# Short convolution and gated feed-forward on one core: the last eviction of a unit shared between two engines, and another order of turns in the last unit

## The chip, the cores and the metric

The kernel runs on one core of one Trainium2 chip. The metric is the device time of one execution in microseconds, and less is better. TensorE (PE) multiplies matrices into PSUM, ScalarE (ACT) and VectorE (DVE) read PSUM, GpSimd (POOL) works on SBUF alone, and SyncE (SP) issues most of the DMA transfers.

## The reference

The input is `x` with 8 batches of 4096 tokens and 192 channels. The first stage is a causal convolution over 7 tokens whose taps are a softmax over 7 weights, one set for each of 8 heads of 24 channels. The second stage is a feed-forward layer with 1536 hidden channels and a gate:

```python
out = np.einsum('hk,bskhg->bshg', softmax(weight), x_unf)   # x_unf: 7 shifted copies of x
x = out.reshape(B * S, D)                                   # 32768 x 192
gate = np.maximum(x @ w_gate, 0.0)
val = x @ w_val
return (gate * val @ w_out)                                 # 32768 x 192
```

## The kernel before

The schedule is written out by hand: every engine executes its instructions in the order in which the program issues them. The 8 batches are taken as 4 pairs, two streams `st` that lie on the upper and the lower 64 partitions. A unit is 1024 tokens of one pair (two windows of 512), and there are 16 units, `u` from 0 to 15.

A unit has two phases on TensorE. First `gate_val` runs for each of its two windows. For each of 12 slices `f` of the hidden channels, 6 matmuls with `Wg` and 6 with `Wv` (line 505) fill two PSUM tiles. ScalarE applies the relu to the gate tile (line 514), and VectorE multiplies the result by the value tile into `hT` (line 515). Each PSUM tile `ps` is two banks of 512 fp32, and the pool has four of them, used in rotation. A slice takes two tiles, so slice `f` reuses the tiles of slice `f - 2`: the value tile of slice 2 is the one that VectorE reads for slice 0.

Then `project` multiplies `hT` by `Wo`. The unit has four halves `i` (two windows, two streams), each with one PSUM tile in which four blocks `q` of 128 tokens by 192 channels lie, two to a bank. Each half is done in two turns (`half_pass`, matmuls on line 534). A turn is 96 matmuls, each with 64 of the 128 rows, and runs over the pairs of blocks (0, 2) and (1, 3), one after the other. The two turns exchange the upper and the lower rows, so that matmuls of different rows never write a bank at the same time. Between the first and the second turn of a half an empty instruction on SyncE (line 547) marks that the first is over. The order of (half, turn) is a list in `project` (lines 590 to 594), with its own form for the last unit. Unit 0 does whole halves with all 128 rows (line 554).

After the second turn of a half, `evict` calls `put`: ScalarE copies the whole tile (768 fp32 a partition, line 567) to an `out_s` buffer, of which there are three, and SyncE issues a store of 384 KB (line 568). The last half of the last unit (`final`) takes three tiles, and is evicted in three pieces on ScalarE and VectorE, with three stores.

While TensorE projects unit `u`, VectorE and ScalarE convolve for unit `u + 2` if there is one. In a unit from 1 to 13, VectorE has 18 instructions on line 481 and 5 products on line 454 in `lane_rest`, all issued ahead of `project`. ScalarE has 16 products on line 452 (`product`), spread over the halves in front of their evictions: 5, 5, 5 and 1. GpSimd adds the products (line 458), and its first addition for the next unit is issued at the start of the unit.

Of the kernel before, what the change touches and what calls it, by code (L numbers as in the profile page):

```python
# [15 lines left out]
def kernel(  # L16
# [12 lines left out]
    nc = tc.nc  # L29

    B, S, D = x.shape
# [4 lines left out]
    NB = B // 2  # L36
# [3 lines left out]
    WIN = 512  # L40
# [66 lines left out]
    def stage(p0, rows, st, n_st, jj, n):  # L107
        at = room[p0 : p0 + rows, 0, 0, 0:1]
        dims = [[D * GSUB, n_st], [D, n], [1, D]]
        return bass.AP(  # L110
            tensor=at.tensor,
            offset=at.offset + D * (GSUB * st + jj),
            ap=[at.ap[0]] + [d for d in dims if d[1] > 1],
        )
# [3 lines left out]
    def body(st):  # L118
# [13 lines left out]
        out=spaced[:, :, GAP : GAP + SEG],  # L132
        in_=ones[0:SUB, 0 : KW * SEG].rearrange("p (k s) -> p k s", k=KW),
# [8 lines left out]
        out=stage(PAD, DSUB, 0, 2, 0, 1),  # L142
        in_=bass.AP(
            tensor=x.tensor, offset=x.offset, ap=[[D, DSUB], [NB * S * D, 2], [1, D]]
        ),
# [53 lines left out]
    def summed(out, step, n, at):  # L199
# [15 lines left out]
        out=mx[:], in_=wr[:], axis=mybir.AxisListType.X, op=ALU.max, negate=True  # L215
# [9 lines left out]
        out=over[:],  # L225
# [10 lines left out]
        out=spread[0:SUB, 0, 0:H],  # L236
# [7 lines left out]
    with nc.allow_low_precision("products with one and zero"):  # L244
        nc.vector.tensor_tensor(
            out=diag[:],
# [6 lines left out]
    for a in range(2):  # L253
        for b in range(NSEG):
            nc.tensor.matmul(
                out=(bps, spread)[a][:, a, HB * SEG * b : HB * SEG * (b + 1)],
# [12 lines left out]
    for h in range(H):  # L269
        r = G * h  # L270
        while r < G * (h + 1):
            c, n = r // 64, min(64 - r % 64, G * (h + 1) - r)
            nc.sync.dma_start(
                out=tap[r % 64 : r % 64 + n, c, :],
                in_=taps[h : h + 1, :].unsqueeze(1).to_broadcast([1, n, KW]),
# [166 lines left out]
    def shifted(u, c, k, lane):  # L442
        o = HALO - KW + 1 + k
        if lane:
            return xrs[u][:, c, 128 * TDVE + o : 128 * TDVE + o + LPOOL]
        return xrs[u][:, c, o : o + LDVE]

    def product(engine, u, c, k):
        out = prods[u][:, k, c, :]
        in_, scale = shifted(u, c, k, 1), tap[:, c, k : k + 1]  # L450
        if engine is nc.scalar:
            engine.activation(out=out, in_=in_, func=ACTF.Copy, scale=scale)  # L452
        else:
            engine.tensor_scalar(out=out, in0=in_, scalar1=scale, scalar2=None, op0=ALU.mult)  # L454
# [63 lines left out]
    def slots(final):  # L518
        wide = [psum.tile([128, 2, 512], FP, name="ps")]
        if not final:  # L520
            return wide, [wide[0][:, q // 2, D * (q % 2) : D * (q % 2) + D] for q in range(4)]
        wide += [psum.tile([128, 2, 512], FP, name="ps") for _ in range(2)]
        return wide, [t[:, n, 0:D] for t, n in zip((wide[0], wide[1], wide[0], wide[2]), (0, 0, 1, 0))]

    SYNC = mybir.DependencyInfo(mybir.DependencyClass.Sync, mybir.DependencyReason.DATA)

    def half_pass(h, st, outs, final, turn, after):


        for n, pair in enumerate(((0, 2), (1, 3))):  # L530
            for f in range(NFF):
                for r in range(2):
                    q = pair[r ^ turn]
                    mm = nc.tensor.matmul(  # L534
                        out=outs[q],
                        lhsT=h[64 * r : 64 * r + 64, f, st, 128 * q : 128 * (q + 1)],
                        rhs=Wo[64 * r : 64 * r + 64, f, :],
                        start=(turn == 0 and f == 0 and (n == 0 or final)),
                        stop=(turn == 1 and f == NFF - 1),
                        tile_position=(64 * r, 0),  # L540
                        skip_group_check=True,
                    )
                    if after is not None:
                        tc.add_manual_dep(mm.ins, after.ins.name, SYNC, reason="same banks, other rows")
                        after = None
        if turn == 0:
            done = nc.sync.nop()
            tc.add_manual_dep(done.ins, mm.ins.name, SYNC, reason="first turn over")
            return done

    def half_whole(h, st, outs):
        for q in range(4):
            for f in range(NFF):
                nc.tensor.matmul(  # L554
                    out=outs[q],
                    lhsT=h[:, f, st, 128 * q : 128 * (q + 1)],
                    rhs=Wo[:, f, :],
                    start=(f == 0),
                    stop=(f == NFF - 1),
                )  # L560

    def put(copy, queue, src, row, n, gap, os_=None):
        if os_ is None:
            os_ = opool.tile([128, 4, D], FP, name="out_s")
        m = src.shape[1] if len(src.shape) == 3 else 1
        dst = os_[:, 0:n, :].rearrange("p (a b) d -> p a (b d)", a=m)
        copy(out=dst, in_=src if len(src.shape) == 3 else src.unsqueeze(1))  # L567
        queue.dma_start(
            out=bass.AP(
                tensor=out.tensor,  # L570
                offset=out.offset + row * D,
                ap=[[D, 128], [gap * D, n], [1, D]],
            ),
            in_=os_[:, 0:n, :],
        )

    def evict(wide, row0, final):
        if not final:
            put(nc.scalar.copy, nc.sync, wide[0][:, :, 0 : 2 * D], row0, 4, 128)
            return  # L580
        ends = apool.tile([128, NCH, LDVE], FP, name="acc")
        o = [ends[:, c, 0 : LDVE].rearrange("p (b d) -> p b d", d=D) for c in range(NCH)]
        put(nc.scalar.copy, nc.sync, wide[0][:, :, 0:D], row0, 2, 256, o[0])
        put(nc.vector.tensor_copy, nc.sync, wide[1][:, 0, 0:D], row0 + 128, 1, 128, o[1])
        put(nc.scalar.copy, nc.scalar, wide[2][:, 0, 0:D], row0 + 384, 1, 128, o[2])

    def project(u, hs, work):
        bp, w0 = u * UNIT // S, u * UNIT % S // WIN
        at, done = {}, {}
        order = [(0, 0), (1, 0), (0, 1), (2, 0), (1, 1), (3, 0), (2, 1), (3, 1)]  # L590
        if u == 0:
            order = [(i, 2) for i in range(4)]
        if u == NUNIT - 1:
            order = [(0, 0), (1, 0), (0, 1), (1, 1), (2, 0), (3, 0), (2, 1), (3, 1)]
        for i, turn in order:
            final = u == NUNIT - 1 and i == 3
            h, st = hs[i // 2], i % 2
            if turn != 1:
                at[i] = slots(final)
            if turn:  # L600
                for c, k in work[i]:
                    product(nc.scalar, u + 2, c, k)
            if turn == 2:
                half_whole(h, st, at[i][1])
            else:
                done[i] = half_pass(h, st, at[i][1], final, turn, done.get(i))
            if turn:
                evict(at[i][0], (bp + NB * st) * S + WIN * (w0 + i // 2), final)
            if u == 0 and i == 0:
                conv(3, 0)  # L610
                conv(3, 1)
# [12 lines left out]
    for u in range(NUNIT):  # L624
# [29 lines left out]
        if u + 2 < NUNIT:  # L654
# [4 lines left out]
            cut = [0, 4, 8, 12, 16] if u == 0 else [0, 5, 10, 15, 16]  # L659
            work = [todo[a:b] for a, b in zip(cut, cut[1:])]  # L660
        project(u, hs, work)


# [28 lines left out]
```

## Time and profile before

| | us |
|---|---|
| three runs | 770.40, 770.37, 769.57 |
| median | 770.37 |
| the profiled execution | 769.82 |
| its span, first to last instruction | 767.8 |
| outside the span | 2.02 |

| engine | busy us | share |
|---|---|---|
| TensorE matmul | 762.1 | 99% |
| VectorE | 684.8 | 89% |
| ScalarE | 604.5 | 79% |
| GpSimd | 369.9 | 48% |

The granted TensorE clock was full speed throughout. The four times lie 0.83 us, or 0.11%, apart. In the profile's views a row begins with the start and the duration in microseconds, counted from the start of the span. In the timeline, brackets give the idle time of the engine just before the row and what ended it. A row with a count merges that many instructions.

### The profile page before, as it was taken

What the parts mean: (1) busy time and instruction counts of PE and PEld (TensorE: products, weight loads), DVE (VectorE), ACT (ScalarE), POOL (GpSimd) and SP (SyncE); (2) the same over time, 40 slices, a digit from 0 to 9 for tenths busy, and PEclk for the clock granted to TensorE, in tenths of its full rate; (3) what the DMA queues carried; (4) which work ended last, traced back from release to release, by engine and by line L of the source; (5) the groups of instructions that cost most, each with busy time, mean ns of one, the idle gap of its engine ahead of it and who ended that gap; (6) DMA issues with size and microseconds to landing.
All of it is one profiled execution on the core that took longest, in us unless ns stands there. A gap on an engine that the chain in (4) does not pass through costs nothing.

```text
span 767.8 us, 24842 instructions
## 1 busy us (share of the span) xinstructions
PE 762.1 (99%) x10842; PEld 527.1 (69%) x10842; DVE 684.8 (89%) x729; ACT 604.5 (79%) x733; POOL 369.9 (48%) x212
## 2 busy tenths in 40 slices
PE   8999999999999999999999999999999999999998
PEld 4495675957759576585866858567595775957757
DVE  6999999989999999999999999999998999995590
ACT  6797887888878788887888878788787887874571
POOL 8608638093470926619166290843909346090000
PEclk9999999999999999999999999999999999999999
DMA  8966727180372704428054271712719131200202
GB/s 121 128 107 118 91 89 90 49 126 6 97 80 69 106 23 98 60 85 94 23 111 46 85 91 44 113 24 85 93 44 117 21 94 37 65 22 22 64 2 84
DMA packets 131809, 56.11 MB, mean 73 GB/s; under 512 B 96741, under 2 KB 131701, under 8 KB 131701
## 3 DMA queue, kind: packets, MB, share of 16 engines
q1 hardware_dynamic: 90789, 38.85, 24.4%
q0 software_dynamic: 40768, 15.59, 19.0%
q8 instruction: 84, 1.38, 0.8%
q14 instruction: 24, 0.20, 0.1%
q10 hardware_dynamic: 144, 0.10, 0.0%
HBM read 31.68 MB, written 25.17 MB: 74 GB/s over the span
## 4 chain that ended last, share of the span: by engine, by line
PE 98%; DMA 1%; DVE 0%; ACT 0%; issue 0%; POOL 0%; POOLq 0%
PE ps L505 65%; PE ps L534 31%; PE ps L554 2%; DMA x_h<-in_x_dram 1%; PE ps L333 0%; PE ps L358 0%; DVE hT L515 0%; ACT gr L514 0%; DVE acc L567 0%; POOL spaced L129 0%; POOLq L676 0%
## 5 line engine op out<-in xcount | busy, mean ns | idle before, releaser
L515 DVE TENSOR_TENSOR hT<-gr,ps 128x1024 f16<-128x1024 f16 x384 | 468.4, 1221 | 60.0 <-ACT gr L514 33.4
L514 ACT ACTIVATE gr<-ps 128x1024 f16<-128x1024 f32 x384 | 393.2, 1024 | 100.2 <-PE ps L505 100.2
L458 POOL TENSOR_TENSOR prods<-prods 128x1344 f32<-128x1344 f32 x70 | 212.4, 3034 | 309.8 <-ACT out_s L567 279.3
L505 PE MATMUL ps<-xc,Wv 64*128 64x512 f16 x2304 | 317.3, 376 | 0.2 <-DVE hT L515 0.2
L505 PE MATMUL ps<-xc,Wg 64*128 64x512 f16 x2304 | 317.3, 376 | 0.0
L534 PEld LDWEIGHTS <-hT 64*128 64x128 f16 x5760 | 238.5, 94 | 3.1
L534 PE MATMUL ps<-Wo,hT 64*128 64x192 f16 x5760 | 240.3, 243 | 0.0
L505 PEld LDWEIGHTS <-Wv 64*128 64x128 f16 x2304 | 138.5, 94 | 111.1 <-issue 3.0
L505 PEld LDWEIGHTS <-Wg 64*128 64x128 f16 x2304 | 128.2, 94 | 116.5 <-issue 0.3
L481 DVE SCALAR_TENSOR_TENSOR acc<-x_r,tap,acc 128x576 f32<-128x576 f16 x210 | 154.3, 810 | 1.6 <-ACT acc L469 1.6
L452 ACT ACTIVATE prods<-x_r,tap 128x448 f32<-128x448 f16 x222 | 130.4, 663 | 0.0
L567 ACT COPY out_s<-ps 128x768 f32<-128x768 f32 x63 | 50.6, 803 | 54.3 <-PE ps L534 44.4
L414 POOL DMA_DIRECT2D x_e<-in_x_dram x56 | 45.2, 819 | 3.3 <-POOL x_p L433 3.3
L433 POOL COPY x_p<-x_e 128x1728 f16<-128x1728 f16 x28 | 44.7, 1626 | 1.8 <-DMA x_e<-in_x_dram 1.8
L458 POOL TENSOR_TENSOR xc<-prods 128x1344 f16<-128x1344 f32 x14 | 42.4, 3026 | 1.1
L481 DVE SCALAR_TENSOR_TENSOR xc<-x_r,tap,acc 128x576 f16<-128x576 f16 x42 | 31.7, 809 | 0.0
L469 ACT ACTIVATE acc<-x_r,tap 128x576 f32<-128x576 f16 x42 | 29.4, 767 | 0.0
L454 DVE TENSOR_SCALAR prods<-x_r,tap 128x448 f32<-128x448 f16 x72 | 27.3, 445 | 0.0
L554 PE MATMUL ps<-Wo,hT 128*128 128x192 f16 x192 | 16.2, 246 | 0.0
L554 PEld LDWEIGHTS <-hT 128*128 128x128 f16 x192 | 15.9, 98 | 0.0
L567 DVE COPY acc<-ps 128x192 f32<-128x192 f32 x1 | 0.4, 357 | 14.2 <-PE ps L534 14.2
L333 PEld LDWEIGHTS <-x_h 110*32 110x32 f16 (+3 forms) x240 | 3.2, 92 | 2.6 <-issue 1.3
(51 smaller groups left out, 59.2 us busy)
## 6 DMA issues: line engine op xcount, KB each, us to landing
out_dram<-out_s SPq DMA_DIRECT2D x63, 384.0 KB
x_e<-in_x_dram POOLq DMA_DIRECT2D x34, 192.0 KB, 6.2
x_e<-in_x_dram POOLq DMA_DIRECT2D x22, 240.0 KB, 5.3
x_r<-x_p SPq DMA_TRANSPOSE x126
Wo<-in_moe_w_out_dram POOLq DMA_DIRECT2D x1, 576.0 KB, 10.1
x_h<-in_x_dram POOLq DMA_DIRECT2D x2, 240.0 KB, 7.6
x_h<-in_x_dram POOLq DMA_DIRECT2D x2, 210.0 KB, 5.7
x_h<-in_x_dram POOLq DMA_DIRECT2D x2, 192.0 KB, 8.0
```

The lines of the kernel that those rows point to most:

```text
L414: nc.gpsimd.dma_start(out=xe[:, j : j + n, st, :, :].rearrange("p j c r -> p j (c r)"), in_=bass.AP(tensor=x.tensor, offset=x.offset + (b ...
L433: nc.gpsimd.tensor_copy(out=xp[:, :, :, st, :], in_=xe[:, :, st, :, :])
L452: engine.activation(out=out, in_=in_, func=ACTF.Copy, scale=scale)
L458: nc.gpsimd.tensor_tensor(out=pr[:, 0] if k < KW - 1 else xc[u][:, :, LDVE:UNIT], in0=pr[:, 0], in1=pr[:, k], op=ALU.add,)
L469: nc.scalar.activation(out=accs[u][:, c, :], in_=shifted(u, c, 0, 0), func=ACTF.Copy, scale=tap[:, c, 0:1],)
L481: nc.vector.scalar_tensor_tensor(out=xc[u][:, c, 0:LDVE] if k == KW - 1 else acc[:, c, :], in0=shifted(u, c, k, 0), scalar=tap[:, c, k : k ...
L505: nc.tensor.matmul(out=pss[i][:, st, :], lhsT=W[64 * st : 64 * st + 64, c, 128 * f : 128 * (f + 1)], rhs=xcb[64 * st : 64 * st + 64, c, WI ...
L514: nc.scalar.activation(out=gr[:], in_=pss[0][:], func=ACTF.Relu)
L515: nc.vector.tensor_tensor(out=h[:, f], in0=gr[:], in1=pss[1][:], op=ALU.mult)
L534: mm = nc.tensor.matmul(out=outs[q], lhsT=h[64 * r : 64 * r + 64, f, st, 128 * q : 128 * (q + 1)], rhs=Wo[64 * r : 64 * r + 64, f, :], sta ...
L554: nc.tensor.matmul(out=outs[q], lhsT=h[:, f, st, 128 * q : 128 * (q + 1)], rhs=Wo[:, f, :], start=(f == 0), stop=(f == NFF - 1),)
L567: copy(out=dst, in_=src if len(src.shape) == 3 else src.unsqueeze(1))
```

## The change

Two things change. In units 1 to 14, the eviction of half 3 becomes two copies of one bank each (384 fp32 a partition): the first on ScalarE, the second on VectorE. One store of 384 KB still takes the buffer out. In the last unit the order of turns becomes (0,0) (1,0) (0,1) (2,0) (1,1) (2,3) (3,0) (2,4) (3,1), in place of (0,0) (1,0) (0,1) (1,1) (2,0) (3,0) (2,1) (3,1). Turns 3 and 4 are the two parts of half 2's second turn, the pair (0, 2) and the pair (1, 3), 48 matmuls each. Each part has an eviction of its own on ScalarE, over the columns of its two blocks in both banks, and a store of 192 KB. Half 3 is evicted as before.

```diff
-    def half_pass(h, st, outs, final, turn, after):
-        for n, pair in enumerate(((0, 2), (1, 3))):
+    def half_pass(h, st, outs, final, turn, after, part=(0, 1)):
+        for n in part:
+            pair = (n, n + 2)
             for f in range(NFF):
...
-        copy(out=dst, in_=src if len(src.shape) == 3 else src.unsqueeze(1))
+        src = src if len(src.shape) == 3 else src.unsqueeze(1)
+        copies = copy if isinstance(copy, tuple) else (copy,)
+        step = m // len(copies)
+        for j, one in enumerate(copies):
+            one(out=dst[:, step * j : step * j + step], in_=src[:, step * j : step * j + step])
         queue.dma_start(
...
-    def evict(wide, row0, final):
+    def evict(wide, row0, final, shared):
         if not final:
-            put(nc.scalar.copy, nc.sync, wide[0][:, :, 0 : 2 * D], row0, 4, 128)
+            copy = (nc.scalar.copy, nc.vector.tensor_copy) if shared else nc.scalar.copy
+            put(copy, nc.sync, wide[0][:, :, 0 : 2 * D], row0, 4, 128)
             return
...
         if u == NUNIT - 1:
-            order = [(0, 0), (1, 0), (0, 1), (1, 1), (2, 0), (3, 0), (2, 1), (3, 1)]
+            order = [(0, 0), (1, 0), (0, 1), (2, 0), (1, 1), (2, 3), (3, 0), (2, 4), (3, 1)]
         for i, turn in order:
...
-            if turn != 1:
+            if turn in (0, 2):
                 at[i] = slots(final)
-            if turn:
+            if turn in (1, 2):
                 for c, k in work[i]:
                     product(nc.scalar, u + 2, c, k)
+            if turn > 2:
+                n = turn - 3
+                half_pass(h, st, at[i][1], final, 1, done.pop(i, None), (n,))
+                put(
+                    nc.scalar.copy,
+                    nc.sync,
+                    at[i][0][0][:, :, D * n : D * n + D],
+                    (bp + NB * st) * S + WIN * (w0 + i // 2) + 128 * n,
+                    2,
+                    256,
+                )
+                continue
...
-                evict(at[i][0], (bp + NB * st) * S + WIN * (w0 + i // 2), final)
+                evict(at[i][0], (bp + NB * st) * S + WIN * (w0 + i // 2), final, u > 0 and i == 3)
```

## The prediction, made before the changed kernel was run

> **What bounds the kernel now.** I read the page first. Its engine line says that TensorE leaves almost nothing free:
>
> ```profile
> PE 762.1 (99%) x10842; PEld 527.1 (69%) x10842; DVE 684.8 (89%) x729; ACT 604.5 (79%) x733; POOL 369.9 (48%) x212
> ```
>
> The chain of waits shows where the rest can be. It runs on TensorE from unit to unit, and ends after its last matmul:
>
> ```profile
> 106.48 31.14 PE ps L505 x288
> ...
> 717.10 31.13 PE ps L505 x288
> 748.23 15.87 PE ps L534 x384
> 764.10 0.02 issue
> 764.12 0.36 DVE acc L567
> ```
>
> Each `gate_val` phase from unit 2 to unit 15 takes 31.13 or 31.14. A change that leaves TensorE's matmuls alone can win only what these phases hold above the matmuls' own pace, and the end after 764.10. So I read the timeline where unit 1 passes to unit 2, engine by engine:
>
> ```profile
> 105.35 1.90 DVE L454 TENSOR_SCALAR prods<-x_r,tap 128x448 f32<-128x448 f16 x5
> 108.32 3.71 DVE L515 TENSOR_TENSOR hT<-gr,ps 128x1024 f16<-128x1024 f16 x3 [1.07 <-ACT gr L514]
> ...
> 106.56 0.80 ACT L567 COPY out_s<-ps 128x768 f32<-128x768 f32 x1 [0.66 <-ACT prods L452]
> 107.26 1.03 ACT L514 ACTIVATE gr<-ps 128x1024 f16<-128x1024 f32 x1
> 108.46 1.02 ACT L514 ACTIVATE gr<-ps 128x1024 f16<-128x1024 f32 x1 [0.17 <-PE ps L505]
> 109.75 1.02 ACT L514 ACTIVATE gr<-ps 128x1024 f16<-128x1024 f32 x1 [0.27 <-PE ps L505]
> 111.10 1.02 ACT L514 ACTIVATE gr<-ps 128x1024 f16<-128x1024 f32 x1 [0.32 <-PE ps L505]
> ...
> 108.25 0.81 PE L505 MATMUL ps<-xc,Wv 64*128 64x512 f16 x6
> 108.90 0.81 PE L505 MATMUL ps<-xc,Wg 64*128 64x512 f16 x6
> 109.59 0.82 PE L505 MATMUL ps<-xc,Wv 64*128 64x512 f16 x6
> ```
>
> Groups of six matmuls start 0.65 apart, except that the value group of slice 2 starts 0.69 after its gate group. It needs the PSUM tile that VectorE reads for slice 0. That multiplication starts at 108.32 and lasts 1.22 (page: mean 1221 ns), so it ends at 109.54, just when the group is due (109.55). It is late because the relu of slice 0 is: ScalarE copies half 3 from 106.56, and takes the relu up at 107.26. A relu that TensorE alone releases starts 0.85 after its gate group (108.90 to 109.75). For slice 0, whose group starts at 106.31, that is 107.16, so the copy costs 0.10 of delay. What TensorE loses shows on ScalarE: relus are 1.295 apart (111.10 to 137.00 is 20 steps), but 109.75 to 111.10 is 1.35, so 0.055. The chain agrees: 24 steps of 1.295 are 31.08 of the 31.13. All 14 phases after units 1 to 14 have this length.
>
> For the end, the timeline and the stretches:
>
> ```profile
> 762.13 0.80 ACT L567 COPY out_s<-ps 128x768 f32<-128x768 f32 x1 [5.14 <-PE ps L534]
> ...
> 763.62 1.23 SPq L568 DMA_DIRECT2D out_dram<-acc  x2
> ...
> 764.44 0.39 ACTq L568 DMA_DIRECT2D out_dram<-acc  x1
> ```
>
> ```profile
> 763.00:763.80 0.80, 0.80 (x24) 0.80 (x21) 0.00 (x0) 0.48 (x1) 0.00 (x0) 1.00 0.00 0
> ...
> 764.00:765.00 1.00, 0.07 (x2) 0.00 (x0) 0.36 (x1) 0.32 (x1) 0.00 (x0) 1.00 1.01 326
> 765.00:766.00 1.00, 0.00 (x0) 0.00 (x0) 0.00 (x0) 0.00 (x0) 0.00 (x0) 1.00 1.03 321
> ...
> 766.20:766.40 0.20, 0.00 (x0) 0.00 (x0) 0.00 (x0) 0.00 (x0) 0.00 (x0) 1.00 0.68 208
> ```
>
> The last two columns are the DMA engines' share and GB/s. From about 763.9 to 766.34 all sixteen are full. They carry half 2 (384 KB) and half 3 (192 + 96 + 96 KB): 786 KB at 325 GB/s is 2.42 us. The last stores are issued near 764.5 but queue behind half 2.
>
> **The eviction in two, units 1 to 14.** ScalarE loses 14 copies of 0.80 and gains 14 of 384 elements; the row for that size is `acc<-ps 128x384` at 763.12, 0.48. VectorE gains 14 copies. Its own rows from PSUM take 0.357 for 192 elements (line 567) and about 0.69 for 512 (line 343), so 384 take about 0.56. The built order of the changed kernel shows what the diff does not: the VectorE copy waits for ScalarE's semaphore, not TensorE's. So the copies run one after the other. ScalarE's ends at 106.56 + 0.48 = 107.04. VectorE is at its products until 105.35 + 1.90 = 107.25 anyway, so this new wait costs nothing; in unit 14 VectorE is free and copies right after ScalarE. The copy then runs to 107.81. Behind it on VectorE stands slice 0's multiplication, which must wait for the relu (107.16 + 1.03 = 108.19), so 0.38 is spare. TensorE's value group of slice 1 reuses half 3's tile and is due at 108.25, so 0.44 is spare (0.89 before). SyncE's store of half 3 leaves some 0.4 later; behind it on SyncE stand the transposes of `x_p`, which GpSimd makes only from 110.39, so that is hidden.
>
> The multiplication then starts at 108.22 and ends at 109.44, 0.11 ahead of the group due at 109.55. The next slice stays clear too: its relu is TensorE's (108.46), its multiplication ends by 110.74, and the group is due at 110.84. So the whole stall goes: 14 x 0.055 = **0.77 us**. Bounds: nothing, if another wait steps in, and 0.77, as no more is there.
>
> **The last unit.** Matmuls neither come nor go. The turns last 1.98 each (15.84 / 8) from 748.23. Half 0 is evicted at 754.2 as before, half 1 at 758.1 instead of 756.2, half 2's first part at 759.1 and its second at 762.1. The waits moved: (2,3) starts at 758.13 and needs the mark of (2,0), set at 756.15. (3,1) starts at 762.09 and needs the mark of (3,0), which SyncE can give at 761.10, since the store queued ahead of it is out at about 760.0. (3,0) takes half 1's tile in its second pair at 760.1, and half 1's eviction is over at 758.97. In the built order (2,4) waits for ScalarE too, which is half 2's first copy, over at 759.6 against 761.1. Every spare is over 0.9 us, so TensorE pays nothing.
>
> At the end, 192 KB are gone to the store before. The second part's copy (0.48 instead of 0.80) ends at 762.61. A store's data starts about 0.94 after its issue (half 0: issued at 755.03, moving from 755.97), so its 192 KB move from 763.6 to 764.2. Half 3's 192 KB, issued at 763.62, move from 764.56 to 765.17. The last two, issued near 764.51, move from 765.45 and take 0.61: to 766.06 instead of 766.34. That is **0.28 us**, at most 0.4 if the ragged end of the packets shortens as well, and at least nothing.
>
> A rule of the Trainium skill, "DMA: Bandwidth & Descriptors", Anatomy of one DMA, speaks against this half: each DMA pays about 2.0 us for setup and receipt, and bytes / 436 GB/s. By it, as an estimate, the last store would land at 764.51 + 2.0 + 0.23 = 766.74 whatever is queued ahead, and the second half of the change would bring nothing. No run here yet shows a last store with free engines ahead of it.
>
> **Sum.** 769.82 - 0.77 - 0.28 = 768.77, so 768.8. That is against the profiled execution, whose time lies 0.55 below the median of the runs (770.37) and 0.22 below the mean of all four (770.04). The 2.02 us outside the span stay.
>
> **The rivals.**
>
> *The end is the last store's own.* The span runs on for 3.3 us after the last issue at 764.5. If that is the store's own time from issue to receipt, the shorter queue gains nothing: 769.82 - 0.77 = 769.05. For it: the store has to wait 0.94 for its first byte in any case. Against it: the engines' share is 1.01 to 1.03 until the end, so data is what they wait for. 12%. The rule of the skill above is this case.
>
> *The stall stays.* VectorE's copy lengthens to some 0.95, or the tile that it holds keeps slice 1's value group (over 0.44 late), and TensorE loses its 0.05 as before: 769.82 - 0.28 = 769.5. Against it: no row of such a size on VectorE is over 0.69. 12%.
>
> *Slower: VectorE's copy meets GpSimd.* GpSimd's first addition starts at 107.42 and takes 3.02, and the new copy would run beside it. If the copy had to let the addition through, it would end at 107.42 + 3.02 + 0.56 = 111.0. Slice 0's multiplication would start 2.7 later than now, 13 times (unit 15 has no additions): 35 us, some 805. It decides from a copy longer than 1.04 (107.25 to 108.29, where the present multiplication is released); every ns beyond that is lost 14 times, so a copy of 1.15 already gives +1.5. Against it: VectorE's cast from PSUM at 20.00 took 0.68 beside a GpSimd copy on line 180 that ran until 20.13, no longer than the others. 8% for all of this side. The Trainium skill, "SBUF — State Buffer", Who interferes with whom, states that a copy in a two-port mode and GpSimd block each other fully, whoever issues first, but that one with at most one SBUF input outside these modes does not contend; the cast at 20.00 agrees with the exception.
>
> **How the numbers follow.** About 0.2%, 1.54 us, is what a measurement of this kernel can tell from no change. My sum is a gain of 1.05 within one execution; but the median of before stands high among its four times, and 768.8 is 1.57 below it. So the main case, 68%, is split by where the runs fall: 43% faster, 25% same. The store's own time gives 4% and 8%, the stall that stays 1% and 11%, the collision 8% slower. That makes 48% faster, 44% same, 8% slower. The range goes from 768.0 (1.17 off the fastest run is 768.4, and as much again as the runs scatter) to 770.1 (the stall stays, the slowest of the runs); the collision alone is outside.
>
> **What would show it.** Right: relu of slice 0 starts 0.85 after its gate group in units 2 to 15; phases of 31.08; VectorE's copy of about 0.56 from 107.25; the DMA share falls below 1 between 764 and 766, and the last data moves by 766.1. Wrong: a value group late after VectorE's copy, a last turn that starts after 762.1 less the gains, or a span that still ends 3.7 after the last matmul.

## The result, and the profile after

The changed kernel takes 768.44 us (median of 19 runs, 768.13 to 770.06), the kernel before 769.86 (19 runs, 769.19 to 771.18). The ratio is 0.9983, with a 95% interval of 0.9976 to 0.999: a gain of about 1.3 us, between 0.8 and 1.8. It is clear of no change, and just below the 1.54 us that the prediction set as its bound for "faster".

The page after, its engine line:

```profile
PE 761.7 (99%) x10842; PEld 502.6 (66%) x10842; DVE 691.8 (90%) x743; ACT 601.1 (78%) x734; POOL 369.8 (48%) x212
```

VectorE has 14 instructions more and ScalarE one more; TensorE's count is the same. (A correction to the sections on the kernel and the change: a turn has 48 matmuls, not 96, and a part 24; the chain counts 384 for the eight turns of a unit. No time above hangs on it.) The chain of waits after:

```profile
59.20 31.19 PE ps L505 x288
...
106.23 31.08 PE ps L505 x288
...
716.19 31.08 PE ps L505 x288
747.27 15.88 PE ps L535 x384
763.15 0.02 issue
763.17 0.36 DVE acc L572
```

All 14 phases of units 2 to 15 are down from 31.13 to 31.08, which is 24 steps of 1.295, TensorE's own pace. The phase of unit 1, which follows an unshared eviction, keeps its 31.19 (what that means comes out below, with the shared eviction in unit 0). Two rows of the kernel before, for comparison: unit 1's phase, and the gate group of slice 0 in unit 2:

```profile
59.45 31.19 PE ps L505 x288
...
106.31 0.81 PE L505 MATMUL ps<-xc,Wg 64*128 64x512 f16 x6
```

The timeline after, where unit 1 passes to unit 2, each engine on its own:

```profile
106.31 0.48 ACT L572 COPY out_s<-ps 128x384 f32<-128x384 f32 x1 [0.66 <-ACT prods L452]
106.92 1.02 ACT L514 ACTIVATE gr<-ps 128x1024 f16<-128x1024 f32 x1
108.21 1.02 ACT L514 ACTIVATE gr<-ps 128x1024 f16<-128x1024 f32 x1 [0.27 <-PE ps L505]
...
105.10 1.90 DVE L454 TENSOR_SCALAR prods<-x_r,tap 128x448 f32<-128x448 f16 x5
106.92 0.55 DVE L572 COPY out_s<-ps 128x384 f32<-128x384 f32 x1
107.97 5.11 DVE L515 TENSOR_TENSOR hT<-gr,ps 128x1024 f16<-128x1024 f16 x4 [0.50 <-ACT gr L514]
...
106.06 0.81 PE L505 MATMUL ps<-xc,Wg 64*128 64x512 f16 x6
...
108.01 0.81 PE L505 MATMUL ps<-xc,Wv 64*128 64x512 f16 x6
108.65 0.81 PE L505 MATMUL ps<-xc,Wg 64*128 64x512 f16 x6
109.30 0.81 PE L505 MATMUL ps<-xc,Wv 64*128 64x512 f16 x6
...
107.17 3.03 POOL L458 TENSOR_TENSOR prods<-prods 128x1344 f32<-128x1344 f32 x1 [17.07 <-DVE prods L454]
```

The relu of slice 0 starts 0.86 after its gate group (106.06 to 106.92), where it was 0.95 (106.31 to 107.26); a relu that TensorE alone releases starts 0.85 to 0.86 after its group. The value group of slice 2 starts 0.65 after the gate group ahead of it, like the others. VectorE's copy runs into what was idle time, and 0.50 of it is left before the multiplication. The end of the span, in stretches (the last two columns are the DMA engines' share and GB/s):

```profile
763.20:763.40 0.20, 0.00 (x0) 0.00 (x0) 0.20 (x1) 0.20 (x1) 0.00 (x0) 1.00 0.24 73
763.40:763.60 0.20, 0.00 (x0) 0.00 (x0) 0.13 (x1) 0.06 (x1) 0.00 (x0) 1.00 0.14 46
763.60:764.20 0.60, 0.00 (x0) 0.00 (x0) 0.00 (x0) 0.00 (x0) 0.00 (x0) 1.00 0.95 307
764.20:764.40 0.20, 0.00 (x0) 0.00 (x0) 0.00 (x0) 0.00 (x0) 0.00 (x0) 1.00 0.14 39
764.40:764.80 0.40, 0.00 (x0) 0.00 (x0) 0.00 (x0) 0.00 (x0) 0.00 (x0) 1.00 0.96 311
764.80:765.00 0.20, 0.00 (x0) 0.00 (x0) 0.00 (x0) 0.00 (x0) 0.00 (x0) 1.00 0.97 296
765.00:765.20 0.20, 0.00 (x0) 0.00 (x0) 0.00 (x0) 0.00 (x0) 0.00 (x0) 1.00 0.15 42
```

Where the engines were full from 764 to 766 before, there are now two holes: they wait for the next store instead of the stores for them. From the last matmul to the end of the span it takes 766.5 - 763.15 = 3.35, where it was 767.8 - 764.10 = 3.70. (The page gives a span to a tenth; the trace itself has 766.49 and 767.81, which makes 3.34 and 3.71. The ends below are worked out with the trace's digits.)

The trace also holds the events by which a store reports that it has landed, which no view here lists. SyncE's last store took 2.29 from issue to landing before (764.51 to 766.80), queued behind the others, and takes 1.98 now (763.56 to 765.54). The span ends about 1 us after this landing in both (1.01 and 0.95).

The profiled executions lie 1.58 apart (769.82 and 768.24), more than the two terms give. Unit 1's phase starts 0.25 earlier (59.45 to 59.20), the 14 phases give 0.70, the end 0.35, and 0.27 lies outside the span (2.02 to 1.75, with the span at 766.49). The first and the last of these are scatter between executions: the kernels are the same up to unit 1, and in the runs below that phase starts anywhere between 58.98 and 59.32, once at 60.81.

### The profile page after: what moved, and what is told of

Read it like the earlier page. It is cut to its first block, busy times and chain, and to the rows that moved or that the text cites. A ratio compares the mean times of both kernels' runs of the same rounds, so it can differ in the third digit from the quotient of the medians.

```text
span 766.5 us, 24874 instructions
## 1 busy us (share of the span) xinstructions
PE 761.7 (99%) x10842; PEld 502.6 (66%) x10842; DVE 691.8 (90%) x743; ACT 601.1 (78%) x734; POOL 369.8 (48%) x212
## 4 chain that ended last, share of the span: by engine, by line
PE 98%; DMA 1%; DVE 0%; ACT 0%; issue 0%; POOL 0%; POOLq 0%
PE ps L505 65%; PE ps L535 31%; PE ps L555 2%; DMA x_h<-in_x_dram 1%; PE ps L333 0%; PE ps L358 0%; DVE hT L515 0%; ACT gr L514 0%; DVE acc L572 0%; POOL spaced L129 0%; POOLq L694 0%
## 5 line engine op out<-in xcount | busy, mean ns | idle before, releaser
L505 PE MATMUL ps<-xc,Wv 64*128 64x512 f16 x2304 | 311.8, 376 | 0.2 <-DVE hT L515 0.2
L505 PE MATMUL ps<-xc,Wg 64*128 64x512 f16 x2304 | 311.9, 376 | 0.0
L505 PEld LDWEIGHTS <-Wv 64*128 64x128 f16 x2304 | 129.9, 94 | 118.8 <-issue 0.5
L505 PEld LDWEIGHTS <-Wg 64*128 64x128 f16 x2304 | 112.2, 94 | 132.4 <-issue 0.2
L572 ACT COPY out_s<-ps 128x768 f32<-128x768 f32 (+1 forms) x64 | 46.1, 721 | 54.0 <-PE ps L535 44.0
L572 DVE COPY out_s<-ps 128x384 f32<-128x384 f32 x14 | 7.7, 549 | 14.8 <-ACT out_s L572 14.8
```

The lines of the kernel that those rows point to most:

```text
L505: nc.tensor.matmul(out=pss[i][:, st, :], lhsT=W[64 * st : 64 * st + 64, c, 128 * f : 128 * (f + 1)], rhs=xcb[64 * st : 64 * st + 64, c, WI ...
L572: one(out=dst[:, step * j : step * j + step], in_=src[:, step * j : step * j + step])
```

## The experiments

**Each part alone.** The first kernel keeps the old order of turns in the last unit:

```diff
-            order = [(0, 0), (1, 0), (0, 1), (2, 0), (1, 1), (2, 3), (3, 0), (2, 4), (3, 1)]
+            order = [(0, 0), (1, 0), (0, 1), (1, 1), (2, 0), (3, 0), (2, 1), (3, 1)]
```

> The shared eviction of units 1 to 14, with the last unit's order of turns as before. My theory: the relu of slice 0 starts 0.86 after its gate group, the 14 phases of gate_val in units 2 to 15 take 31.08 instead of 31.13, so about 0.70 less than before; the end is as before, 3.70 from the last matmul to the end of the span. Rival (the gain comes from the end alone): phases of 31.13, no gain.

It took 768.64, ratio 0.9991 (0.9982 to 1.0). Its chain of waits:

```profile
106.11 31.08 PE ps L505 x288
...
747.15 15.88 PE ps L535 x384
763.04 0.02 issue
```

The phases are at 31.08, and the span, 766.73 in the trace, leaves 3.69 after the last matmul. The second kernel keeps ScalarE's whole eviction:

```diff
-            copy = (nc.scalar.copy, nc.vector.tensor_copy) if shared else nc.scalar.copy
+            copy = nc.scalar.copy
```

> The new order of turns and the two parts in the last unit, with ScalarE alone evicting half 3 in units 1 to 14. My theory: the 14 phases stay at 31.13, the end shrinks from 3.70 to about 3.34, so about 0.36 less than before. Rival (the last store's own time sets the end): the end stays at 3.70, no gain at all.

It took 769.21, ratio 0.9996 (0.9987 to 1.0005), which by itself tells nothing. The chain of waits does:

```profile
716.97 31.13 PE ps L505 x288
748.10 15.87 PE ps L535 x384
```

The phases stay at 31.13. The last matmul ends at 763.97 and the span at 767.34, so the end is 3.37. Both rivals fall: the parts are separate, one gives the phases, the other the end. The times alone would not show it, the traces do; the product of the two ratios, 0.9987, agrees with 0.9983 within the intervals.

**Are the two copies side by side?** The built order had shown the second copy waiting for the first. Exchanging the engines tells whether the wait counts:

```diff
-            copy = (nc.scalar.copy, nc.vector.tensor_copy) if shared else nc.scalar.copy
+            copy = (nc.vector.tensor_copy, nc.scalar.copy) if shared else nc.scalar.copy
```

> As the changed kernel, but VectorE copies the first bank and ScalarE the second, in units 1 to 14. Theory that the two copies run one after the other: ScalarE must now wait for VectorE, which is at its products until 0.94 after the start of slice 0's gate group; ScalarE's copy then ends 1.9 after that start, the relu of slice 0 starts 0.9 to 1.0 later than in the changed kernel, and the phases after units 1 to 13 grow by 0.8 to 0.9 (31.9 to 32.0), that after unit 14 by about 0.2: 11 to 12 us more than the changed kernel. Rival (a bank each means that they run side by side, and the order of the two names is without effect): phases of 31.08, the time of the changed kernel.

It took 780.83, ratio 1.0149 (1.0135 to 1.0163), 12.4 more than the changed kernel and a little more than expected. Its timeline at the same place:

```profile
107.56 0.48 ACT L572 COPY out_s<-ps 128x384 f32<-128x384 f32 x1 [1.85 <-DVE out_s L572]
107.94 2.96 ACT L514 ACTIVATE gr<-ps 128x1024 f16<-128x1024 f32 x3
...
106.98 0.55 DVE L572 COPY out_s<-ps 128x384 f32<-128x384 f32 x1
109.00 2.35 DVE L515 TENSOR_TENSOR hT<-gr,ps 128x1024 f16<-128x1024 f16 x2 [1.47 <-ACT gr L514]
...
106.12 0.81 PE L505 MATMUL ps<-xc,Wg 64*128 64x512 f16 x6
...
108.09 0.82 PE L505 MATMUL ps<-xc,Wv 64*128 64x512 f16 x6
109.02 0.82 PE L505 MATMUL ps<-xc,Wg 64*128 64x512 f16 x6
110.27 0.82 PE L505 MATMUL ps<-xc,Wv 64*128 64x512 f16 x6 [0.43 <-DVE hT L515]
```

ScalarE sits idle for 1.85 until VectorE, busy with its products, has made its copy (106.98 to 107.53). The relu of slice 0 starts 1.82 after its gate group (106.12) instead of 0.86, and TensorE loses its time at both groups of slice 2: the gate group comes 0.28 late and the value group another 0.60. The phases after units 1 to 13 take 32.00 and the one after unit 14 takes 31.41, which adds up to 12.3. So two copies pay in one order of the two names only: the engine that is needed next, here ScalarE for the relu, must come first.

**How much room VectorE has.** First the whole tile on VectorE:

```diff
-            copy = (nc.scalar.copy, nc.vector.tensor_copy) if shared else nc.scalar.copy
+            copy = nc.vector.tensor_copy if shared else nc.scalar.copy
```

> As the changed kernel, but VectorE copies the whole of half 3 in units 1 to 14, ScalarE nothing of it. The copy of 768 elements should take 0.96 and end some 1.87 after the start of slice 0's gate group; half 3's tile is due for the value group of slice 1 at 1.95, slice 0's multiplication at 1.91. My theory (spare of 0.38 and 0.44 behind the half copy): just hidden, phases of 31.08 to 31.13, so within 0 to 0.7 of the changed kernel. Rival (VectorE has no room behind its products): the copy delays the multiplication by its added 0.4, phases of 31.4 or more, over 4 us more than the changed kernel.

It took 768.7, ratio 0.9991 (0.9983 to 1.0), and all 14 phases are at 31.08. Its timeline:

```profile
107.02 0.95 DVE L572 COPY out_s<-ps 128x768 f32<-128x768 f32 x1
108.07 3.81 DVE L515 TENSOR_TENSOR hT<-gr,ps 128x1024 f16<-128x1024 f16 x3
...
108.10 0.81 PE L505 MATMUL ps<-xc,Wv 64*128 64x512 f16 x6
```

The copy ends at 107.97, 0.13 before the value group of slice 1 that needs the tile: hidden, with nearly all of the room used. So the gain in the phases does not need the halving: to give VectorE the whole copy wins the same 0.70, with less room left. Then the half copy three times over:

```diff
-            one(out=dst[:, step * j : step * j + step], in_=src[:, step * j : step * j + step])
+            for _ in range(3 if j else 1):
+                one(out=dst[:, step * j : step * j + step], in_=src[:, step * j : step * j + step])
```

> As the changed kernel, but VectorE makes its copy of the second bank three times in units 1 to 14. The copies should end 2.4 to 2.6 after the start of slice 0's gate group. Theory (spare of 0.44 until the value group of slice 1 needs the tile, at 1.95): the phases of gate_val grow by 0.5 to 0.7, to 31.6 to 31.8, in total 7 to 10 us more than the changed kernel, and the late group is the value group of slice 1. Rival (only the multiplication waits, the tile is free earlier): the late group is the value group of slice 2, by 0.4 to 0.5, some 6 us. Rival (VectorE's idle time hides it): phases of 31.08.

It took 779.37, ratio 1.0125 (1.011 to 1.014), 10.9 more than the changed kernel. Its timeline:

```profile
106.84 1.74 DVE L573 COPY out_s<-ps 128x384 f32<-128x384 f32 x3
108.50 2.34 DVE L515 TENSOR_TENSOR hT<-gr,ps 128x1024 f16<-128x1024 f16 x2
...
105.99 0.81 PE L505 MATMUL ps<-xc,Wg 64*128 64x512 f16 x6
...
107.28 0.81 PE L505 MATMUL ps<-xc,Wg 64*128 64x512 f16 x6
108.64 0.82 PE L505 MATMUL ps<-xc,Wv 64*128 64x512 f16 x6 [0.54 <-DVE out_s L573]
```

The late group is the value group of slice 1, released by VectorE's last copy (108.58) and 0.71 behind its due time of 107.93. So it is the tile that ends the room, as the theory had it, ahead of the multiplication. The copies ended 2.59 after the start of the gate group, at the upper end of what I had put, since each further copy added 0.60. Thirteen losses of 0.71 and one of 0.60, in the last unit, add up to 9.8. The profiled execution, 778.07, is 9.8 above that of the changed kernel; the median of the four runs lies a little above the 7 to 10 expected, by their scatter (778.07 to 779.97).

The same limit in unit 0, where VectorE has seven products and TensorE's projection is shorter:

```diff
-                evict(..., final, u > 0 and i == 3)
+                evict(..., final, i == 3)
```

> As the changed kernel, with the shared eviction in unit 0 too, where VectorE is at its products until some 1.1 us after TensorE's projection ends. Theory (VectorE's products in front of the copy decide whether it is hidden): the phase after unit 0 grows from 31.19 by 0.1 to 0.3, the value group of slice 1 starts late; the time is 0.1 to 0.3 above the changed kernel, too little to time. Rival (halving ScalarE's copy always helps): the phase after unit 0 falls to 31.08, 0.1 less.

It took 768.39, ratio 0.9985 (0.9975 to 0.9994). The phase of unit 1 went from 31.19 to 31.22:

```profile
58.98 31.22 PE ps L505 x288
...
60.28 0.55 DVE L572 COPY out_s<-ps 128x384 f32<-128x384 f32 x1
...
60.22 0.81 PE L505 MATMUL ps<-xc,Wg 64*128 64x512 f16 x6
60.89 0.82 PE L505 MATMUL ps<-xc,Wv 64*128 64x512 f16 x6
```

VectorE's copy ends at 60.83, and the value group of slice 1 starts at 60.89. It was due at 60.87; it starts 0.06 behind the copy that frees its tile, as it does with three copies (108.58 to 108.64). So the copy is just not hidden, and costs 0.03 where I expected 0.1 to 0.3. It did not help either, because there is nothing to win behind unit 0. The chain cuts its pieces differently there: in the changed kernel the first gate group of unit 1 starts at 59.13, 0.07 before its piece, and that of unit 2 at 106.06, 0.17 before. Counted from these groups to the end of the phase, unit 1 takes 31.26 and unit 2 takes 31.25. The 31.19 is no stall. The run can't be told from the changed kernel by its time.

**What shortens the end.** The new order of turns, but half 2 in one copy and one store of 384 KB after its second part:

```diff
-                put(nc.scalar.copy, nc.sync, at[i][0][0][:, :, D * n : D * n + D], ..., 2, 256)
+                if turn == 4:
+                    evict(at[i][0], (bp + NB * st) * S + WIN * (w0 + i // 2), False, False)
```

> As the changed kernel, with the new order of turns in the last unit, but half 2 is copied and stored in one piece (384 KB) after its second part. Theory that the queue ahead of the last stores sets the end: the engines are full from about 0.3 before the last matmul, and the end is 3.6 to 3.7 after the last matmul as before, some 0.3 more than the changed kernel. Rival (the order of turns brings the shorter end, not the smaller store): the end stays at 3.34. Rival (the last store's own time sets the end): 3.34 as well.

It took 768.72, ratio 0.9991 (0.9982 to 1.0001). The last matmul ends at 764.76 and the span at 768.46, so the end is 3.70 again, and the engines are full to the end:

```profile
764.70:765.70 1.00, 0.02 (x2) 0.00 (x0) 0.36 (x1) 0.32 (x1) 0.00 (x0) 1.00 1.03 326
765.70:766.70 1.00, 0.00 (x0) 0.00 (x0) 0.00 (x0) 0.00 (x0) 0.00 (x0) 1.00 1.04 323
```

So the order of turns alone brings nothing; the 192 KB that left earlier do. (The profiled execution also lost 1.6 us in unit 0, where the kernels are alike.) Last, half 2's second turn whole and ahead of half 3's first:

```diff
-            order = [(0, 0), (1, 0), (0, 1), (2, 0), (1, 1), (2, 3), (3, 0), (2, 4), (3, 1)]
+            order = [(0, 0), (1, 0), (0, 1), (2, 0), (1, 1), (2, 1), (3, 0), (3, 1)]
```

> As the changed kernel, but half 2's second turn is not split: it runs whole before half 3's first turn, so that half 2's store is some 2 us earlier still, and nothing lies between half 3's two turns. The changed kernel's end is no longer set by the queue (its DMA share is 0.51 just before the last stores), so no more is won there: 3.3 to 3.4 from the last matmul to the end. TensorE must wait for the mark between half 3's turns: 0.1 to 0.3 us lost, so 0 to 0.3 more than the changed kernel in total. Rival (the queue still counts): the end shrinks by another 0.2 or more.

It took 768.63, ratio 0.9988 (0.9979 to 0.9998), not to be told from the changed kernel by its time. Its chain of waits:

```profile
747.09 13.88 PE ps L535 x336
761.00 0.05 issue
761.04 2.20 PE ps L535 x48
```

The stretch before the last stores' data, and TensorE's weight loads (PEld) between half 3's turns:

```profile
762.60:763.60 1.00, 0.60 (x16) 0.37 (x10) 0.33 (x1) 0.45 (x2) 0.00 (x0) 1.00 0.00 0
...
761.04 1.93 PEld L535 LDWEIGHTS <-hT 64*128 64x128 f16 x48 [0.33 <-SPq L548]
```

The span ends at 766.65, 3.41 after the last matmul at 763.24. All of half 2 is gone early and no data moves from 762.60 to 763.60, yet the end is no shorter than with half of it left. SyncE's last store again takes 1.98 from issue to landing (763.65 to 765.64). So what is queued ahead counts no more; the last stores' own time is left. And between half 3's turns, which need the mark on line 548, the weight loads stand still for 0.33. In the chain TensorE waits 0.05, and the last turn then takes 2.20 instead of 1.98: the projection lasts 16.15 (747.09 to 763.24) instead of 15.88. Laying a part of half 2's turn between them saves these 0.27.

## Why the prediction was right

- **What bounds.** Right, in its place and its count: slice 0's relu behind ScalarE's copy, its multiplication, the value group of slice 2, 14 times. With the copy halved all 14 went, and with ScalarE's whole copy (the second experiment) all 14 stayed.
- **The stall.** I took 0.055 from one pair of relus and wrote 0.77; the phases show 0.05, so 0.70. The prediction had both figures: the chain's 31.13 - 31.08 is 0.05, and I took the larger one.
- **The wait on ScalarE.** Costed at nothing, because VectorE is at its products anyway. It cost nothing: VectorE's copy starts at 106.92, at the end of its products, and 0.13 after ScalarE's copy is over (106.79). With the engines exchanged the same wait is worth 12 us.
- **VectorE's copy.** 0.56 from its neighbours, 0.55 measured (541 to 558 ns over the 14). Of the room behind it I put 0.38 ahead of the multiplication and 0.44 ahead of the tile's group; 0.50 and 0.54 were there, mostly because VectorE takes it up 0.08 before the products' row ends. The tile is the one that would end it, shown by three copies; one of 0.95 still fits.
- **The last unit.** TensorE lost nothing to the moved waits (15.88 against 15.87). The end gave about 0.35, where I had 0.28 and at most 0.4. The size was off because the last data moved until about 765.03, 1.88 after the last matmul, and I had put it at 1.96. ScalarE's store is issued at 763.49 and its data starts at about 764.37, 0.88 later; I had counted 0.94, and from SyncE's issue, which is 0.07 later.
- **The rivals.** That the last store's own time sets the end was false before the change, and is what is left after it: the queue ahead was worth 0.31 of the 2.29 that the last store took. The collision with GpSimd did not come: its addition started at 107.17, beside the copy, and both kept their durations: 3.03 for the addition, and 0.55 for the copy, which takes 0.56 in unit 14 with no addition beside it. They ran together for only 0.30. This agrees with the exception that I cited from the Trainium skill, "SBUF — State Buffer", Who interferes with whom. The rule of the Trainium skill, "DMA: Bandwidth & Descriptors", Anatomy of one DMA, gives 2.23 for the last store, as an estimate; in the changed kernel 1.98 was measured, with the landing. What I drew from the rule, that the second half of the change would bring nothing, did not come. The section gives its figure for DMAs that GpSimd issues; these stores are issued by SyncE and ScalarE.
- **The sum.** 0.70 + 0.35 = 1.05, as predicted, but that the sum is met to the last digit is luck: 0.07 too much for the stall cancels 0.07 too little for the end. The measured ratio gives 1.3, with 0.8 to 1.8 as its interval, so nothing is missing that these runs could show. The split of the main case between faster and same was about this scatter.

## What to carry to other kernels

When an engine on the path does its last copy of one stage ahead of the first work of the next, look for another engine that idles just there, and give that engine the second half: the copies may run in turn, if the one that is needed next goes first. Where its room is large enough, the whole copy does as well. Find the room of the helper from both consumers, its own next instruction and the next writer of the buffer that it holds. At the end of a kernel, look at whether the transfer engines are full until the last byte. Here, while they were, what was queued ahead of the last stores counted (0.35), and once holes had appeared it no longer did.

## What the runs showed that was not expected

A copy that follows other work on VectorE started 0.08 before the row ahead of it ended (106.92, with products until 107.00), while three copies that write the same place one after another were 0.60 apart, though each lasts 0.55 to 0.56. That they wait for each other is argued from this gap, not shown. On rooms of half a microsecond both matter.
